# Retention attention and a two-layer FFN on one core: both matrix products by one level of Strassen, with attention and weight rounding as a first part

## The chip, the core and the metric

The kernel runs on one core of a Trainium2 chip. A core has a matrix engine (TensorE, PE in the profile; its weight loads are listed apart as PEld), a vector engine (VectorE, DVE), a scalar engine (ScalarE, ACT), GpSimd (POOL) and a queue that only issues transfers (SyncE, SP). Operands lie in SBUF, matrix results in PSUM: 8 banks of 512 fp32 values in each of 128 partitions. The metric is the device time of one execution in microseconds.

## The reference, cut to what matters

The inputs q, k, v are float32 of 8 batches x 8 heads x 576 positions x 64. The two weight matrices reach the kernel as 8-byte doubles, and the kernel rounds them to float32 itself.

```python
scores = scale * np.matmul(q, k.transpose(0, 1, 3, 2))        # scale = 1/8
gamma = 1.0 - 2.0 ** (-5.0 - np.arange(H))                    # one decay per head
Dmat = np.where(rel >= 0, gamma[:, None, None] ** rel, 0.0)   # rel = i - j
attn_out = np.matmul(scores * Dmat[None], v)
x = attn_out.transpose(0, 2, 1, 3).reshape(B * S, H * D)      # 4608 x 512
h = x @ w_in                                                  # 512 x 2048
sp = np.maximum(h, 0.0) + np.log1p(np.exp(-np.abs(h)))        # softplus
g = h * erf(sp)
return g @ w_out                                              # 2048 x 512
```

## The kernel before

**Attention.** Each batch is cut into pieces of 128 positions (four full ones and one of 64): 40 pieces, 32 full and 8 short. For a piece, `transposes` brings q and k into [feature, position] form by TensorE and copies them out with ScalarE; `scores` makes the 8 heads' score blocks and VectorE multiplies them with a triangle into `sT`; `outputs` makes scores x v, adds the part of earlier positions by a running state (`old`, 128 x 128 per pair of heads), scales the result by the decays into a column block of `xT`, and updates the state by k^T v with two or three VectorE operations (L275 to L278). GpSimd weighs the next piece's keys (L193).

**FFN.** Tokens are taken in 9 chunks of 512. For a chunk, `hidden` (L304) makes h^T in 8 groups of two 128-row tiles of d_ff: per tile 4 float32 products, 128 x 128 weights against 512 columns, into half of a 2-bank PSUM tile `ph`. `serf` (L316) applies Softplus and Erf on ScalarE (each with its own table load) and the product with h on VectorE. `project` (L326) makes the output of the *previous* chunk, 128 tokens at a time, again with 512 columns per product. A float32 product is two MATMUL and two LDWEIGHTS instructions on TensorE: 9 chunks x 64 products x 2 = 1152 records for each of the two matrix products.

**Weight rounding.** The doubles come in 32 parts of 128 x 512 (512 KB each, four in flight). A part costs two ScalarE, five VectorE (L159 to L170) and two GpSimd operations (L171, L172).

**The order of the work** is the program's own, each engine's queue in the order of the code. Pieces 0 to 3 come first, with the first parts of w_in. Then for each chunk c and group g four quarters run: half of `hidden` of chunk c, a step of `project` of chunk c-1, and after each quarter `attend` issues the stages of attention that are due for chunk c+1. The rest of w_in is rounded in chunk 0 and all of w_out by the start of chunk 1. So attention, rounding and matrix products share the engines for the first chunks, and attention and products to the end.

Of the kernel before, what the change touches and what calls it, by code (L numbers as in the profile page):

```python
# [18 lines left out]
P = 128  # L19
# [3 lines left out]
CONST_COLS = H + 2 * NP * P + P  # L23
# [7 lines left out]
def decays():  # L31


    gamma = 1.0 - 2.0 ** (-5.0 - np.arange(H, dtype=np.float64))
    t = np.arange(P)
    gk = gamma[None, :] ** (-t[:, None])
    row = gamma.reshape(NP, 2).repeat(D, axis=1).T
    gq = row[:, :, None] ** t[None, None, :] / math.sqrt(D)
    same = (t[:, None] // D) == (t[None, :] // D)
    gs = (row**P)[:, :, None] * same[:, None, :]  # L40
    tri = t[None, :] >= t[:, None]
    return np.concatenate([gk, gq.reshape(P, -1), gs.reshape(P, -1), tri], axis=1).astype(np.float32)
# [3 lines left out]
def kernel(  # L46
# [13 lines left out]
    TCH = 512  # L60
    n_ch = n_tok // TCH
    n_dc = D_MODEL // P
    n_ft = D_FF // P
    GF = 2
    n_g = n_ft // GF
    W = GF * TCH
    PREFETCH = 2
    WP = 512
    WAHEAD = 4

    const = ctx.enter_context(tc.tile_pool(name="const", bufs=1))
    raw = ctx.enter_context(tc.tile_pool(name="raw", bufs=PREFETCH + 2))
    att = ctx.enter_context(tc.tile_pool(name="att", bufs=2))
    xpool = ctx.enter_context(tc.tile_pool(name="xpool", bufs=3))
    gpool = ctx.enter_context(tc.tile_pool(name="gpool", bufs=12))
    opool = ctx.enter_context(tc.tile_pool(name="opool", bufs=2))
    ps_at = ctx.enter_context(tc.tile_pool(name="ps_at", bufs=2, space=PSUM))
    ps_h = ctx.enter_context(tc.tile_pool(name="ps_h", bufs=2, space=PSUM))
    ps_o = ctx.enter_context(tc.tile_pool(name="ps_o", bufs=1, space=PSUM))
# [4 lines left out]
    loaded = {}  # L84

    def load(i):
        if i >= len(pieces):
            return
        b, s0, n = pieces[i]
        t = {}  # L90
        for name, src in (("k", k), ("q", q), ("v", v)):
            t[name] = raw.tile([P, H, D], FP32, tag=name, name=f"raw_{name}")
            nc.sync.dma_start(out=t[name][:n], in_=src[b, :, s0 : s0 + n, :].rearrange("h p d -> p h d"))
        loaded[i] = t

    load(0)
    cst = const.tile([P, CONST_COLS], FP32, name="cst")
    nc.scalar.dma_start(out=cst, in_=consts)
    gk = cst[:, 0:H]
    gq = cst[:, H : H + NP * P].rearrange("p (a i) -> p a i", a=NP)  # L100
    gs = cst[:, H + NP * P : H + 2 * NP * P].rearrange("p (a i) -> p a i", a=NP)
    tri = cst[:, H + 2 * NP * P : CONST_COLS]
    for i in range(1, PREFETCH):
        load(i)


    w_in_sb = const.tile([P, n_dc, D_FF], FP32, name="w_in_sb")
    w_out_sb = const.tile([P, n_ft, D_MODEL], FP32, name="w_out_sb")

    def parts_in(g):  # L110

        f = g * GF * P
        step = WP // (GF * P)
        for dc in range(0, n_dc, step):
            src = w_in[dc * P : (dc + step) * P, :].rearrange("(c p) f -> p c f", p=P)
            yield w_in_sb[:, dc : dc + step, f : f + GF * P], src, slice(f, f + GF * P)

    def parts_out(g):
        for ft in range(g * GF, (g + 1) * GF):
            src = w_out[ft * P : (ft + 1) * P, :].rearrange("(c p) f -> p c f", p=P)  # L120
            yield w_out_sb[:, ft : ft + 1, :], src, slice(0, D_MODEL)

    parts = [p for g in range(n_g) for p in parts_in(g)] + [p for g in range(n_g) for p in parts_out(g)]
    N_IN = len(parts) // 2
    words = []
    rounded = [0]

    def load_weights():
        if len(words) < len(parts):
            dst, src, cols = parts[len(words)]  # L130
            t = None
            if w_in.dtype == FP32:
                nc.sync.dma_start(out=dst, in_=src[:, :, cols])
            else:
                t_f = gpool.tile([P, W], FP32, tag="g", name="wraw")
                t = t_f[:, :].bitcast(UINT32).rearrange("p (c f) -> p c f", c=dst.shape[1])
                nc.sync.dma_start(out=t, in_=src[:, :, 2 * cols.start : 2 * cols.stop])
            words.append(t)

    def round_weights(upto):  # L140


        while rounded[0] < min(upto, len(parts)):
            n = rounded[0]
            rounded[0] += 1
            dst = parts[n][0]
            t = words[n]
            if t is None:
                load_weights()
                continue  # L150
            pairs = t.rearrange("p c (f two) -> p c f two", two=2)
            pairs_f = t.bitcast(FP32).rearrange("p c (f two) -> p c f two", two=2)
            low, high = pairs[:, :, :, 0], pairs[:, :, :, 1]
            r_f, high_f = pairs_f[:, :, :, 0], pairs_f[:, :, :, 1]
            a_f, a = dst, dst.bitcast(UINT32)
            nc.scalar.activation(a_f, high_f, AF.Abs)
            nc.scalar.mul(out=r_f, in_=low, mul=2.0**-52)

            nc.vector.tensor_scalar(  # L159
                out=a_f, in0=a_f, scalar1=HIGH_LEAST, scalar2=HIGH_MOST, op0=ALU.max, op1=ALU.min  # L160
            )
            nc.vector.tensor_scalar(  # L162
                out=a, in0=a, scalar1=3, scalar2=0x7FFFFFFF, op0=ALU.logical_shift_left, op1=ALU.bitwise_and
            )
            nc.vector.scalar_tensor_tensor(  # L165
                out=a, in0=high, scalar=0x80000000, in1=a, op0=ALU.bitwise_and, op1=ALU.bitwise_or
            )
            nc.vector.tensor_scalar(out=a, in0=a, scalar1=0x40000000, scalar2=None, op0=ALU.bitwise_xor)

            nc.vector.tensor_scalar(out=high, in0=a, scalar1=0xFF800000, scalar2=None, op0=ALU.bitwise_and)  # L170
            nc.gpsimd.tensor_tensor(out=r_f, in0=high_f, in1=r_f, op=ALU.mult)  # L171
            nc.gpsimd.tensor_tensor(out=a_f, in0=a_f, in1=r_f, op=ALU.add)  # L172
            load_weights()

    for _ in range(WAHEAD):
        load_weights()

    ident = const.tile([P, P], FP32, name="ident")
    make_identity(nc, ident)


    xts = {}
    live = {}
    state = {"prev": None}
# [4 lines left out]
    def weigh_keys(i):  # L189

        if i < len(pieces):
            n, t = pieces[i][2], loaded[i]["k"]
            nc.gpsimd.tensor_tensor(  # L193
                out=t[:n], in0=t[:n], in1=gk[:n].unsqueeze(2).to_broadcast([n, H, D]), op=ALU.mult
            )

    def transposes(i):
        n = pieces[i][2]
        t = live[i] = loaded.pop(i)
        load(i + PREFETCH)  # L200
        weigh_keys(i + 1)
        for name in "qk":
            pt = ps_at.tile([P, NP, P], FP32, tag="at", name=f"pt_{name}")
            for p in range(NP):
                nc.tensor.transpose(pt[:, p, :n], flat(t[name][:n, 2 * p : 2 * p + 2, :]), ident[:n, :n])  # L205
            t[name + "T"] = att.tile([P, NP, P], FP32, tag=name + "T", name=name + "T")
            nc.scalar.copy(out=t[name + "T"][:, :, :n], in_=pt[:, :, :n])  # L207

    def scores(i):
        n, t = pieces[i][2], live[i]  # L210
        sT = t["sT"] = att.tile([P, 2, NP, P], FP32, tag="sT", name="sT")
        ps = [ps_at.tile([P, NP, P], FP32, tag="at", name=f"s{e}") for e in range(2)]
        for p in range(NP):
            for e in range(2):
                r = slice(e * D, (e + 1) * D)
                nc.tensor.matmul(  # L216
                    ps[e][:n, p, :n], lhsT=t["kT"][r, p, :n], rhs=t["qT"][r, p, :n], start=True, stop=True
                )
        for e in range(2):
            nc.vector.tensor_tensor(  # L220
                out=sT[:n, e, :, :n],
                in0=ps[e][:n, :, :n],
                in1=tri[:n, :n].unsqueeze(1).to_broadcast([n, NP, n]),
                op=ALU.mult,
            )

    def outputs(i):
        b, s0, n = pieces[i]
        t = live.pop(i)
        old = state["prev"] if s0 > 0 else None  # L230
        o = ps_at.tile([P, NP, P], FP32, tag="at", name="o")
        for p in range(NP):
# [20 lines left out]
        while t0 < b * S + s0 + n:  # L253
            c = t0 // TCH
            if c not in xts:
                xts[c] = xpool.tile([P, n_dc, TCH], FP32, tag="xT", name="xT")
# [144 lines left out]
```

## Time and profile before

| | |
|---|---|
| Median of 3 runs | 1274.95 us (1272.73 to 1275.04) |
| The profiled execution: its time | 1274.32 us |
| Its span, from first to last instruction | 1272.3 us, so 2.0 us lie outside |
| TensorE busy | 1199.3 us (94%) |
| VectorE / ScalarE / GpSimd busy | 305.2 / 429.8 / 121.0 us |
| Moved by DMA | 55.8 MB, of it 45.68 MB read |
| Mean granted TensorE clock | 0.975 of 2.4 GHz |

Busy time is a share of the span over stages that differ; TensorE's busy time also holds the drain of each instruction, so the distance between two starts, not the duration of one, is what an instruction costs in a stream. The view by stretches (below) tells the stages apart.

### The profile page before, as it was taken

To read this page: it belongs to the slowest core of one execution; us is meant where nothing else is said; L and a number is where in the kernel's file an instruction comes from. 1 tells how busy PE (TensorE), PEld (TensorE's weight loads), DVE (VectorE), ACT (ScalarE), POOL (GpSimd) and SP (SyncE) were. 2 spreads that over 40 slices of the span, in tenths; PEclk is the share of its full clock that TensorE was granted. 3 is DMA by queue.
4 is the path that set the end of the run, shared out by engine and by line. 5 is a ranking of instruction groups with operands and counts; after the bars stand their busy time and mean duration, and the time that the engine had idled before them with its cause. 6 is when DMAs were issued, how large, how long until landed. Compare 5 with 4: busy or idle time off the path is not lost.

```text
span 1272.3 us, 10583 instructions
## 1 busy us (share of the span) xinstructions
PE 1199.3 (94%) x4416; PEld 601.2 (47%) x4416; DVE 305.2 (24%) x412; ACT 429.8 (34%) x469; POOL 121.0 (10%) x110
## 2 busy tenths in 40 slices
PE   5966559999999999999999999999999999999998
PEld 4533334454544544445544554445454454444443
DVE  3379975111111111111211111111111111110000
ACT  2355353333323333333332333333323333243210
POOL 3245543000000000000000000000000000000000
PEclk9887779999999999999999999999999999999999
DMA  9723450001202120101130112011211000000000
GB/s 239 180 75 112 124 127 12 7 25 37 51 4 54 25 53 14 42 13 42 25 67 13 42 25 58 9 30 25 58 34 29 0 17 1 17 1 16 1 18 32
DMA packets 124543, 55.80 MB, mean 44 GB/s; under 512 B 113616, under 2 KB 113616, under 8 KB 124496
## 3 DMA queue, kind: packets, MB, share of 16 engines
q1 hardware_dynamic: 124352, 54.54, 17.2%
q8 instruction: 35, 0.57, 0.2%
q10 hardware_dynamic: 144, 0.59, 0.1%
q14 instruction: 12, 0.10, 0.0%
HBM read 45.68 MB, written 9.44 MB: 43 GB/s over the span
## 4 chain that ended last, share of the span: by engine, by line
PE 85%; DVE 6%; ACT 1%; issue 0%; DMA 0%; POOL 0%; DVEq 0%; ACTq 0%; POOLq 0%
PE po L334 39%; PE ph L308 35%; PE s L216 3%; PE o L234 2%; PE o L244 2%; PE kv L270 2%; DVE w_out_sb L165 1%; PE pt_q L205 1%; PE pt_k L205 1%; DVE w_in_sb L165 1%; DVE w_out_sb L162 1%; DVE w_in_sb L162 1%; DMA wraw<-in_moe_w_out_dram 0%; DVE wraw L170 0%; DVE w_out_sb L159 0%
## 5 line engine op out<-in xcount | busy, mean ns | idle before, releaser
L308 PE MATMUL ph<-xT,w_in_sb 128*128 128x512 f32 x1152 | 530.2, 604 | 20.4 <-DVE xT L259 11.4
L334 PE MATMUL po<-w_out_sb,g 128*128 128x512 f32 x1152 | 518.2, 595 | 0.5 <-ACT osb L343 0.5
L308 PEld LDWEIGHTS ph<-xT,w_in_sb 128*128 128x128 f32 x1152 | 216.9, 193 | 271.2 <-issue 247.0
L334 PEld LDWEIGHTS po<-w_out_sb,g 128*128 128x128 f32 x1152 | 215.7, 190 | 260.9 <-issue 256.9
L320 DVE TENSOR_TENSOR g<-ph,g 128x1024 f32<-128x1024 f32 x72 | 88.2, 1224 | 762.4 <-ACT g L319 623.1
L318 ACT ACTIVATE g<-ph 128x1024 f32<-128x1024 f32 x72 | 73.8, 1024 | 491.2 <-PE ph L308 487.4
L318 ACT ACT_TABLE_LOAD x72 | 92.4, 1283 | 68.5 <-issue 33.0
L193 POOL TENSOR_TENSOR raw_k<-raw_k,cst 128x512 f32<-128x512 f32 (+1 forms) x40 | 42.7, 1071 | 746.7 <-DMA raw_k<-in_k_dram 746.7
L207 ACT COPY qT<-pt_q 128x512 f32<-128x512 f32 (+1 forms) x40 | 21.6, 541 | 216.1 <-PE pt_q L205 216.1
L319 ACT ACT_TABLE_LOAD x72 | 92.4, 1283 | 1.3
L319 ACT ACTIVATE g<-g 128x1024 f32<-128x1024 f32 x72 | 76.1, 1056 | 0.8
L216 PE MATMUL s<-qT,kT 64*128 64x128 f32 (+1 forms) x640 | 48.8, 286 | 21.7 <-DVE xT L259 20.1
L216 PEld LDWEIGHTS s<-qT,kT 64*128 64x128 f32 (+1 forms) x640 | 40.1, 187 | 51.0 <-issue 25.0
L220 DVE TENSOR_TENSOR sT<-s,cst 128x512 f32<-128x512 f32 (+1 forms) x80 | 46.9, 627 | 46.4 <-PE s L216 46.4
L205 PE MATMUL pt_q<-ident,raw_q 128*128 128x128 f32 (+1 forms) x160 | 24.8, 280 | 24.9 <-DVE sT L220 18.1
L234 PEld LDWEIGHTS o<-sT,raw_v 128*64 128x64 f32 (+1 forms) x640 | 33.1, 140 | 29.4 <-issue 25.8
L171 POOL TENSOR_TENSOR wraw<-wraw 128x512 f32<-128x512 f32 x32 | 34.4, 1076 | 107.2 <-issue 61.4
L234 PE MATMUL o<-sT,raw_v 128*64 128x128 f32 (+1 forms) x640 | 42.2, 275 | 1.1 <-ACT qT L207 1.0
L259 DVE TENSOR_TENSOR xT<-o,cst 128x512 f32<-128x512 f32 (+1 forms) x44 | 25.6, 590 | 71.0 <-PE o L244 60.1
L205 PEld LDWEIGHTS pt_q<-ident,raw_q 128*128 128x128 f32 (+1 forms) x160 | 19.2, 148 | 46.5 <-DVE sT L220 21.0
L343 ACT COPY osb<-po 128x512 f32<-128x512 f32 x36 | 19.6, 581 | 55.2 <-PE po L334 55.2
L244 PE MATMUL o<-qT,state 128*128 128x128 f32 (+1 forms) x256 | 37.6, 291 | 0.0
(31 smaller groups left out, 404.6 us busy)
## 6 DMA issues: line engine op xcount, KB each, us to landing
out_dram<-osb SPq DMA_DIRECT2D x36, 256.0 KB, 2.2
raw_k<-in_k_dram SPq DMA_DIRECT2D x32, 256.0 KB, 3.7
raw_q<-in_q_dram SPq DMA_DIRECT2D x32, 256.0 KB, 4.4
raw_v<-in_v_dram SPq DMA_DIRECT2D x32, 256.0 KB, 4.3
wraw<-in_moe_w_in_dram SPq DMA_DIRECT2D x16, 512.0 KB, 5.2
wraw<-in_moe_w_out_dram SPq DMA_DIRECT2D x16, 512.0 KB, 3.2
raw_k<-in_k_dram SPq DMA_DIRECT2D x8, 128.0 KB, 2.9
raw_q<-in_q_dram SPq DMA_DIRECT2D x8, 128.0 KB, 3.5
```

The costliest lines, as they stand in the source:

```text
L171: nc.gpsimd.tensor_tensor(out=r_f, in0=high_f, in1=r_f, op=ALU.mult)
L193: nc.gpsimd.tensor_tensor(out=t[:n], in0=t[:n], in1=gk[:n].unsqueeze(2).to_broadcast([n, H, D]), op=ALU.mult)
L205: nc.tensor.transpose(pt[:, p, :n], flat(t[name][:n, 2 * p : 2 * p + 2, :]), ident[:n, :n])
L216: nc.tensor.matmul(ps[e][:n, p, :n], lhsT=t["kT"][r, p, :n], rhs=t["qT"][r, p, :n], start=True, stop=True)
L220: nc.vector.tensor_tensor(out=sT[:n, e, :, :n], in0=ps[e][:n, :, :n], in1=tri[:n, :n].unsqueeze(1).to_broadcast([n, NP, n]), op=ALU.mult,)
L234: nc.tensor.matmul(o[e * D : (e + 1) * D, p, :n], lhsT=t["v"][:n, 2 * p + e, :], rhs=t["sT"][:n, e, p, :n], start=(p == 0), stop=(old is N ...
L244: nc.tensor.matmul(o[:, p, :n], lhsT=old[:, p, :], rhs=t["qT"][:, p, :n], start=False, stop=(p == NP - 1), skip_group_check=True,)
L308: nc.tensor.matmul(ph[:, j * TCH : (j + 1) * TCH], lhsT=w_in_sb[:, dc, f : f + P], rhs=xts[c][:, dc, :], start=(dc == 0), stop=(dc == n_dc ...
L318: nc.scalar.activation(t, ph, AF.Softplus)
L319: nc.scalar.activation(t, t, AF.Erf)
L320: nc.vector.tensor_tensor(out=t, in0=ph, in1=t, op=ALU.mult)
L334: nc.tensor.matmul(po[tt], lhsT=t[:, j * TCH + tt * P : j * TCH + (tt + 1) * P], rhs=w_out_sb[:, ft, :], start=(ft == 0), stop=(ft == n_ft ...
```

## The change

**Strassen.** Each matrix product is split into 2 x 2 blocks and made with 7 block products in place of 8, in the form with 15 block sums (Winograd's), where partial sums stay in PSUM from one block product to the next. For h^T the blocks are halves of d_model and of d_ff against halves of d_model and halves of the chunk's 512 tokens; for the output they are halves of d_ff, of the tokens and of the 512 output columns. All matrix instructions thereby have 256 columns. For a chunk and each of 4 groups the first product has 7 block products of 4 float32 products each; the second has 7 block products of 16. That is 9 x (4 x 28 + 112) = 2016 float32 products of 256 columns, 4032 MATMUL records, for 1152 float32 products of 512 columns, 2304 records.

The sums of weight blocks (`wa`, `wb`, 7 each) are made once, at rounding, by 4 VectorE operations for each block position (16 of 512 values and 32 of 256 a partition). The sums of x are made once per chunk (4 VectorE operations), the sums of the left operand of the second product once per group (`finish_group`, 4 after the two products with the Erf result).

**Two parts.** Attention for all 40 pieces and the rounding of all 32 parts come first, in three stages one piece apart, with 0.84 parts of rounding per piece; x^T is stored chunk by chunk to DRAM (`xd`, 1 MB each) and SBUF and PSUM are given to the second part. That part loads one chunk of x^T at a time (one buffer, `load_x`), and runs `first_products`, `middle_products`, `last_products`, `serf`, `finish_group` and `multiply2` as the loop at the end writes them. The state of attention now accumulates in PSUM (`kv`) with absolute decays on v and on the output, and ScalarE copies it out; VectorE's state operations and the exclusive-or of the rounding are gone.

```diff
     TCH = 512
+    TH = TCH // 2
...
-    GF = 2
...
+    OH = D_MODEL // 2
+    GP = 2
+    n_g = n_fp // GP
...
-            nc.vector.tensor_scalar(out=a, in0=a, scalar1=0x40000000, scalar2=None, op0=ALU.bitwise_xor)
...
+                load_weights()
+                if sums:
+                    sums[0](*sums[1:])
...
+        def store(upto):
+            while stored[0] < upto:
+                nc.sync.dma_start(out=xd[stored[0]], in_=xts.pop(stored[0]))
+                stored[0] += 1
...
+        for i in range(n_p + 2):
+            if i < n_p:
+                transposes(i)
+            if 0 <= i - 1 < n_p:
+                scores(i - 1)
+            if i >= 2:
+                b, s0, _ = pieces[i - 2]
+                store((b * S + s0) // TCH)
+                outputs(i - 2)
+            round_weights(-(-len(todo) * (i + 1) // (n_p - 2)))
+        store(n_ch)
...
+    def multiply1(c, g, a, acc, start):
+        for j in range(GP):
+            f = (g * GP + j) * P
+            for d in range(2):
+                nc.tensor.matmul(
+                    acc[:, j * TH : (j + 1) * TH],
+                    lhsT=wa[:, a, d, f : f + P],
+                    rhs=x[c][a][:, d, :],
...
+    def first_products(c, g):
...
+        multiply1(c, g, A11, t["a"], True)
+        nc.scalar.copy(out=t["g1"][:, 0], in_=t["a"])
+        multiply1(c, g, A12, t["e"], True)
+        tt(t["g1"][:, 0], t["e"], t["g1"][:, 0], ALU.add)
+
+    def middle_products(c, g):
...
+        multiply1(c, g, S2, t["a"], False)
+        nc.vector.tensor_copy(out=t["g1"][:, 1], in_=t["a"])
+        multiply1(c, g, S3, t["g"], True)
+        multiply1(c, g, S1, t["a"], False)
+        nc.vector.tensor_copy(out=t["g2"][:, 1], in_=t["a"])
+        tt(t["g2"][:, 1], t["g"], t["g2"][:, 1], ALU.add)
+
+    def last_products(c, g):
...
+        multiply1(c, g, S4, t["a"], False)
+        nc.scalar.copy(out=t["g2"][:, 0], in_=t["a"])
+        multiply1(c, g, A22, t["g"], False)
+        tt(t["g1"][:, 1], t["g"], t["g1"][:, 1], ALU.add)
+
+    def serf(c, g):
...
+        for func in (AF.Softplus, AF.Erf):
+            for j in "12":
+                nc.scalar.activation(t["e" + j], t["g" + j] if func == AF.Softplus else t["e" + j], func)
+
+    def finish_group(c, g):
...
+        for j in "12":
+            tt(t["g" + j], t["g" + j], t["e" + j], ALU.mult)
...
+        tt(s1, g12, g22, ALU.add)
+        tt(s2, s1, g11, ALU.subtract)
+        tt(g12, g11, g12, ALU.subtract)
+        tt(s4, g21, s2, ALU.subtract)
...
+    for c in range(n_ch):
+        for g in range(n_g):
+            middle_products(c, g)
+            if g > 0:
+                finish_group(c, g - 1)
+            if g + 1 < n_g:
+                first_products(c, g + 1)
+            else:
+                acc, osb = begin_outputs(c)
+                multiply2(c, B11, acc["a"], True, ALL[: n_g - 2])
+            last_products(c, g)
+            serf(c, g)
+        finish_group(c, n_g - 1)
+        multiply2(c, B11, acc["a"], False, ALL[n_g - 2 : n_g - 1])
+        multiply2(c, B21, acc["e"], True, ALL[: n_g - 1])
+        load_x(c + 1)
+        multiply2(c, B11, acc["a"], False, ALL[n_g - 1 :])
...
+        multiply2(c, B21, acc["e"], False, ALL[n_g - 1 :])
...
+        multiply2(c, T2, acc["a"], False, ALL)
...
+        multiply2(c, T3, acc["g"], True, ALL)
+        multiply2(c, T1, acc["a"], False, ALL)
...
+        if c + 1 < n_ch:
+            first_products(c + 1, 0)
+        multiply2(c, B22, acc["a"], False, ALL)
...
+        multiply2(c, T4, acc["g"], False, ALL)
```

On TensorE, in the middle of the kernel before, a quarter's product (`ph`, 4 products of 512 columns), a step of the previous chunk's output (`po`) and a stage of attention (`o`, `kv`) take turns:

```order
L308 MATMUL ph<-xT,w_in_sb 128x512 x4
L334 MATMUL po_2776<-w_out_sb,g 128x512 x2
L334 MATMUL po_2779<-w_out_sb,g 128x512 x2
L234 MATMUL o<-sT,raw_v 64x128 x8
L244 MATMUL o<-qT,state 128x128 x4
L270 MATMUL kv<-raw_v,raw_k 128x128 x4
L308 MATMUL ph<-xT,w_in_sb 128x512 x4
```

In the changed kernel's second part the same engine has block products alone, here of the groups of one chunk (`acc_a`, `acc_e`, `acc_g` are the PSUM sums, `xs` the sums of x):

```order
L362 MATMUL acc_a<-x,wa 128x256 x4
L362 MATMUL acc_e<-x,wa 128x256 x4
L362 MATMUL acc_a<-x,wa 128x256 x4
L362 MATMUL acc_g<-xs,wa 128x256 x4
L362 MATMUL acc_a<-xs,wa 128x256 x4
L362 MATMUL acc_g<-xs,wa 128x256 x4
```

Attention has left these rows, and each accumulator is written again four to sixteen matrix instructions after it was last read or written.

On ScalarE, before, one group's Softplus and Erf stand like this; the table load of Softplus waits for VectorE (a buffer of `g` to come free), the operation itself for TensorE's `ph`:

```order
L318 ACT_TABLE_LOAD [waits DVE_49]
L318 ACTIVATE g<-ph 128x1024 [waits PE_49]
L319 ACT_TABLE_LOAD
L319 ACTIVATE g<-g 128x1024 [waits Activation_49]
```

In the changed kernel, one group of the second part:

```order
L401 COPY g_2986<-acc_a 128x512 [waits DVE_49,PE_49]
L410 ACT_TABLE_LOAD [waits DVE_49]
L410 ACTIVATE e_3073<-g_2985 128x1024 [waits Activation_49]
L410 ACTIVATE e_3074<-g_2986 128x1024 [waits Activation_49]
L410 ACT_TABLE_LOAD
L410 ACTIVATE e_3073<-e_3073 128x1024 [waits Activation_49]
L410 ACTIVATE e_3074<-e_3074 128x1024 [waits Activation_49]
```

The input of Softplus now comes from VectorE (the sum that ends `last_products`), and the wait for it stands at the table load, not behind it.

On TensorE at the seam of the two products of a chunk, changed kernel, with what the first instruction of each waits for (`g_3157` is the last group's left operand, `oa` and `oe` the sums of the output):

```order
L432 MATMUL oa<-wb,g_3051 128x256 x4
L362 MATMUL acc_a<-x,wa 128x256 [waits DVE_49]
L362 MATMUL acc_a<-x,wa 128x256 x3
L362 MATMUL acc_g<-xs,wa 128x256 [waits DVE_49]
L362 MATMUL acc_g<-xs,wa 128x256 x3
L432 MATMUL oa<-wb,g_3104 128x256 [waits DVE_49]
L432 MATMUL oa<-wb,g_3104 128x256 x3
L432 MATMUL oe<-wb,g_2985 128x256 x4
L432 MATMUL oe<-wb,g_3051 128x256 x4
L432 MATMUL oe<-wb,g_3104 128x256 x4
L432 MATMUL oa<-wb,g_3157 128x256 [waits DVE_49]
```

Between the last group's first product (`acc_g`) and the first instruction that reads this group's result (`oa<-wb,g_3157`) there stand 16 float32 products.

## Rows read from the trace of the kernel before

**Rows 1.** The page: span, and busy time of the engines.

```profile
span 1272.3 us, 10583 instructions
PE 1199.3 (94%) x4416; PEld 601.2 (47%) x4416; DVE 305.2 (24%) x412; ACT 429.8 (34%) x469; POOL 121.0 (10%) x110
```

**Rows 2.** Stretches: us, busy (count) per engine, granted clock, DMA share, GB/s.

```profile
core 0: us, PE busy (x) PEld busy (x) DVE busy (x) ACT busy (x) POOL busy (x), PEclk, DMA share, GB/s
20.00:40.00 20.00, 16.08 (x143) 12.83 (x139) 13.54 (x24) 3.90 (x7) 7.61 (x7) 0.97 0.91 202
40.00:60.00 20.00, 19.18 (x90) 11.83 (x91) 6.79 (x12) 7.45 (x10) 4.33 (x5) 0.86 0.78 207
...
100.00:120.00 20.00, 14.16 (x69) 8.94 (x70) 18.76 (x28) 7.53 (x13) 9.68 (x8) 0.73 0.37 102
...
300.00:600.00 300.00, 300.00 (x1126) 149.74 (x1125) 51.16 (x66) 99.45 (x105) 10.40 (x10) 1.00 0.14 33
```

**Rows 3.** Groups by line: records, busy us, mean ns, idle time before.

```profile
L308 PE MATMUL ph<-xT,w_in_sb 128*128 128x512 f32 x1152 | 530.2, 604 | 20.4 <-DVE xT L259 11.4 <-POOL w_in_sb L172 9.0
L334 PE MATMUL po<-w_out_sb,g 128*128 128x512 f32 x1152 | 518.2, 595 | 0.5 <-ACT osb L343 0.5
```

**Rows 4.** Timeline of the weight loads: start, us, line, idle before.

```profile
607.97 0.97 PEld L270 LDWEIGHTS kv<-raw_v,raw_k 128*128 128x128 f32 x8
...
612.41 0.19 PEld L308 LDWEIGHTS ph<-xT,w_in_sb 128*128 128x128 f32 x1 [0.24 <-issue]
612.84 0.19 PEld L308 LDWEIGHTS ph<-xT,w_in_sb 128*128 128x128 f32 x1 [0.24 <-issue]
```

**Rows 5.** Timeline of TensorE's matrix instructions in the middle.

```profile
607.09 1.16 PE L244 MATMUL o<-qT,state 128*128 128x128 f32 x8
608.08 1.06 PE L270 MATMUL kv<-raw_v,raw_k 128*128 128x128 f32 x8
608.98 3.60 PE L334 MATMUL po<-w_out_sb,g 128*128 128x512 f32 x8
...
615.94 1.16 PE L216 MATMUL s<-qT,kT 64*128 64x128 f32 x16
```

**Rows 6.** Timeline of TensorE over the opening pieces.

```profile
24.82 0.66 PE L205 MATMUL pt_q<-ident,raw_q 128*128 128x128 f32 x4 [0.58 <-DVE sT L220]
...
31.80 0.66 PE L205 MATMUL pt_q<-ident,raw_q 128*128 128x128 f32 x4 [0.58 <-DVE sT L220]
...
37.61 2.02 PE L216 MATMUL s<-qT,kT 64*128 64x128 f32 x16 [1.34 <-DVE xT L259]
...
43.17 2.08 PE L244 MATMUL o<-qT,state 128*128 128x128 f32 x8
```

**Rows 7.** DMA queues: packets, MB, their time as share of 16 engines' span.

```profile
q1 hardware_dynamic: 124352, 54.54, 17.2%
```

**Rows 8.** Groups by line and shape, VectorE and GpSimd.

```profile
L320 DVE TENSOR_TENSOR g<-ph,g 128x1024 f32<-128x1024 f32 x72 | 88.2, 1224 | 762.4 <-ACT g L319 623.1 <-PE po L334 139.2
L172 POOL TENSOR_TENSOR w_in_sb<-w_in_sb,wraw 128x512 f32<-128x512 f32 x16 | 21.7, 1355 | 1.3
L278 DVE TENSOR_TENSOR state<-state,cst 128x512 f32<-128x512 f32 x24 | 16.8, 700 | 0.8
L168 DVE TENSOR_SCALAR w_in_sb<-w_in_sb 128x512 uint32<-128x512 uint32 x16 | 6.8, 427 | 0.5
```

**Rows 9.** Timeline of TensorE after a pause at 124 us.

```profile
126.07 1.75 PE L216 MATMUL s<-qT,kT 64*128 64x128 f32 x16 [2.11 <-DVE xT L259]
127.75 5.35 PE L308 MATMUL ph<-xT,w_in_sb 128*128 128x512 f32 x8
```

**Rows 10.** Timeline of ScalarE over one group in the middle.

```profile
599.96 1.28 ACT L318 ACT_TABLE_LOAD   x1
606.17 1.02 ACT L318 ACTIVATE g<-ph 128x1024 f32<-128x1024 f32 x1 [4.93 <-PE ph L308]
...
608.50 1.06 ACT L319 ACTIVATE g<-g 128x1024 f32<-128x1024 f32 x1
```

**Rows 11.** Timeline of the end.

```profile
1268.13 0.59 ACT L343 COPY osb<-po 128x512 f32<-128x512 f32 x1 [1.13 <-PE po L334]
```

More of the change, by code (lines that the diff above doesn't have):

```diff
@@ L73 @@
[L73 to L79, printed above, removed]
+    wa = const.tile([P, 7, 2, D_FF // 2], FP32, name="wa")
@@ L80 @@
+    A11, A12, S3, A22, S1, S2, S4 = range(7)
+    wb = const.tile([P, 7, n_fp, OH], FP32, name="wb")
+    B11, T3, B21, B22, T1, T2, T4 = range(7)
+    xd = [dram.tile([P, n_dc, TCH], FP32, tag="xd", name="xd") for _ in range(n_ch)]
     ctx.enter_context(tc.manual_schedule())
     pieces = [(b, s0, min(P, S - s0)) for b in range(B) for s0 in range(0, S, P)]
[L84 to L167, printed above, removed]
-            nc.vector.tensor_scalar(out=a, in0=a, scalar1=0x40000000, scalar2=None, op0=ALU.bitwise_xor)
[L170 to L173, printed above, removed]
@@ L209, in scores @@
[L209 to L215, printed above, removed]
-                nc.tensor.matmul(
[L217 to L225, printed above, removed]
@@ new lines, with load_x @@
+    ps_2 = ctx.enter_context(tc.tile_pool(name="ps_2", bufs=1, space=PSUM, reuse_waits="tile"))
+    x = {}
+    def load_x(c):
+        if c >= n_ch:
+            return
+        t = xpool.tile([P, n_dc, TCH], FP32, tag="x", name="x")
+        nc.sync.dma_start(out=t, in_=xd[c])
+        s = xpool.tile([P, 4, 2, TH], FP32, tag="xs", name="xs")
+        b11, b12, b21, b22 = (t[:, 2 * d : 2 * d + 2, h * TH : (h + 1) * TH] for d in range(2) for h in range(2))
+        t1, t2, t3, t4 = (s[:, j] for j in range(4))
+        tt(t1, b12, b11, ALU.subtract)
+        tt(t2, b22, t1, ALU.subtract)
+        tt(t3, b22, b12, ALU.subtract)
+        tt(t4, b21, t2, ALU.subtract)
+        x[c] = {A11: b11, A12: b21, S4: b22, A22: t4, S1: t1, S2: t2, S3: t3}
@@ L266, in outputs @@
-        if s0 + n < S:
-            kv = ps_at.tile([P, NP, P], FP32, tag="at", name="kv")
-            for p in range(NP):
-                h = slice(2 * p, 2 * p + 2)
-                nc.tensor.matmul(
-                    kv[:, p, :], lhsT=flat(t["k"][:n, h, :]), rhs=flat(t["v"][:n, h, :]), start=True, stop=True
-                )
-            new = att.tile([P, NP, P], FP32, tag="state", name="state")
-            if old is None:
-                nc.vector.tensor_tensor(out=new, in0=kv, in1=gs, op=ALU.mult)
-            else:
-                nc.vector.tensor_tensor(out=new, in0=kv, in1=old, op=ALU.add)
-                nc.vector.tensor_tensor(out=new, in0=new, in1=gs, op=ALU.mult)
-            state["prev"] = new
@@ L282 @@
-    stages = [(transposes, 0)]
-    for i in range(len(pieces)):
-        stages.append((scores, i))
-        if i + 1 < len(pieces):
-            stages.append((transposes, i + 1))
-        stages.append((outputs, i))
-    done = [0]
-    def stages_for(tokens):
-        last = max(i for i, (b, s0, _) in enumerate(pieces) if b * S + s0 < tokens)
-        return stages.index((outputs, last)) + 1
-    def attend(upto):
-        while done[0] < min(upto, len(stages)):
-            of, i = stages[done[0]]
-            of(i)
-            done[0] += 1
@@ L302 @@
-    gs_of = {}
-    def hidden(c, g, js, ph):
-        for j in js:
-            f = (g * GF + j) * P
-            for dc in range(n_dc):
-                nc.tensor.matmul(
-                    ph[:, j * TCH : (j + 1) * TCH],
-                    lhsT=w_in_sb[:, dc, f : f + P],
-                    rhs=xts[c][:, dc, :],
-                    start=(dc == 0),
-                    stop=(dc == n_dc - 1),
-                )
-    def serf(c, g, ph):
-        t = gs_of[c, g] = gpool.tile([P, W], FP32, tag="g", name="g")
-        nc.scalar.activation(t, ph, AF.Softplus)
-        nc.scalar.activation(t, t, AF.Erf)
-        nc.vector.tensor_tensor(out=t, in0=ph, in1=t, op=ALU.mult)
@@ L347 @@
[L347 to L370 removed]
+    W = GP * TH
@@ new lines, in multiply2 @@
+    def multiply2(c, a, acc, start, gs):
+        for g in gs:
+            left = groups[c, g]["left"][a]
+            for j in range(GP):
+                for tp in range(2):
+                    nc.tensor.matmul(
+                        acc[:, tp, :],
+                        lhsT=left[:, j * TH + tp * P : j * TH + (tp + 1) * P],
+                        rhs=wb[:, a, g * GP + j, :],
+                        start=(start and g == 0 and j == 0 and tp == 0),
+                        stop=(g == n_g - 1 and j == GP - 1),
+                        skip_group_check=True,
+                    )
```

361 lines of the change are left out of this document (245 added, 116 removed).

## The prediction

> **What bounds the kernel now.** I read the page's busy times first, then the stretches, then the timelines of TensorE and its weight loads. The page says TensorE 94% busy, the next engine a third [rows 1]. The stretches say where the rest is: from 300 to 600 us TensorE is busy for all 300 us at full clock, while in the opening it had 16.1 and 19.2 of 20 us, and at 100 us 14.2 of 20 at a granted 0.73 of 2.4 GHz beside a VectorE busy for 18.8 [rows 2]. So in the steady state TensorE's instruction stream is the time, and over the first chunks VectorE's rounding and waits for attention hold it.
>
> What an instruction costs in the stream is the distance of two starts. Weight loads of the FFN stand 0.43 us apart (612.41, 612.84), 0.19 busy and 0.24 idle [rows 4]; a run of 8 lasts 3.60 with its drain [rows 5]. With 1152 records in each product [rows 3], the FFN needs 2304 x 0.43 = 991 us of TensorE. The other 1272.3 - 991 = 281 us are attention's matrix instructions (busy 1199.3 - 530.2 - 518.2 = 151 us [rows 1, 3]), slow clock and idle time.
>
> **The matrix products.** 2304 records of 512 columns go, 4032 of 256 columns come. No row has 256 columns, so I bound it. From below it is half of 0.43, 0.215 us, if only columns count. From above it is twice a 128-column instruction: 8 of them lie 0.99 us apart (607.09 to 608.08), 0.124 each, which gives 0.248 [rows 5]. The next 8 take 0.90 (608.08 to 608.98), 0.112 each, with weight loads end to end for 0.97 us, 0.12 a load [rows 4, 5]. So at 128 columns loads and columns are near level, and at 256 the load has twice the room. The straight line from 0.112 at 128 to 0.43 at 512 gives 0.218 at 256; the lower bound 0.215. I take 0.217: 4032 x 0.217 = 875 us, with ends of 867 and 1000. That is 116 less than now.
>
> A load of 0.12 to 0.19 us hides behind 0.21 us of columns only if loads run beside matrix instructions that use the whole array. In the FFN's rows they do: 0.43 is 512 columns and no more, load included [rows 4]. The Trainium skill says otherwise ("TensorE: Matmul & The Clock Gate", section "Measured speedup vs the span model"): weight loads overlap matrix instructions in flight only where the row group differs. All products here use all rows, so by that rule 0.43 would have been load plus columns, and the trace differs. What the rule would make of the time is the third rival.
>
> **The first part.** All of attention and rounding now run without FFN under them. Its resources, by rows:
> - DMA: before, the hardware queue moved 54.54 MB in 17.2% of the span, 219 us, 249 GB/s with all engines at work [rows 7]. The first part moves as much: the same 45 MB of input, and 9.4 MB of x^T where 9.4 MB of output was. At the 202 and 207 GB/s of the busy opening [rows 2] it is 266 us. I take the middle, 245.
> - VectorE: 305.2 - 88.2 (L320) = 217 us belong to attention and rounding now [rows 1, 8]. Off go 56 state operations at 0.70 and 32 exclusive-ors at 0.43 (39 + 14); on come the weight sums, 16 at 0.70 and 32 of half the width at 0.35 (11 + 11). That leaves 186 us. At 12 places the sums wait for GpSimd to finish the part just rounded, two operations of up to 1.36 [rows 8]: 12 x 2.7 = 32. Together 218.
> - TensorE: 151 us at the clock it had. GpSimd 121 us as now [rows 1].
>
> Four engines within 120 to 245 us, so the slowest sets it if the queues don't make them take turns. Now a piece takes 7.0 us (24.82 to 31.80) because its stages follow each other [rows 6]; the new loop has scores one piece and outputs two pieces behind, so a wait for a copy or for the triangle has a whole piece to pass. Behind a late VectorE sum stands the next triangle, and TensorE waits for that one piece later; that is the coupling I see, and 245 against 218 leaves it some room. The last load is followed by two pieces' stages, some 13 us. First part: 245 + 13 = 258, with ends of 219 + 13 = 232 and 40 x 7.0 + 13 = 293, or worse with a slow clock (second rival).
>
> **The seam of the parts.** The last 1 MB of x^T goes out, the first comes back, nothing beside it: 2.1 MB at 249 GB/s is 8.4, and 9 with VectorE's last operation. Then TensorE starts at half clock: after a pause of 2.11 us 16 score instructions took 1.75 us and 8 FFN ones 5.35, where 1.16 and 3.60 are usual [rows 5, 9]. That is 2.4; I take 3.
>
> **Waits in the second part.** One group is 28 products, 56 records, 12.15 us of TensorE. Beside it VectorE has nine 512-element operations (0.70 each) and two of 1024 (1.22 each) [rows 8], 8.8 us; ScalarE two table loads of 1.28, four operations of 1.02 to 1.06 [rows 10] and two copies of 0.59 [rows 11], 8.0 us. Neither fills the group, but they form a ring: last sum from PSUM (0.7), table load, two Softplus, table load, first Erf (1.28 + 2.05 + 1.28 + 1.06 = 5.7), two products and four sums (about 4.5, since independent ones overlap), the next group's first sum (0.65), the last sum again. With some 0.3 for hand-overs it is 11.9 us against 12.15. TensorE does not wait inside a chunk, by a small margin.
>
> At the chunk's seam it does. Before, the Softplus table load was done at 599.96 while TensorE still worked, 4.9 us ahead of its input [rows 10]; now the order puts the wait for the input at the table load, so its 1.28 us comes after. From the end of the last group's first product: 0.25 drain, 0.7 sum, 5.7 on ScalarE, 1.22 product, 0.3 hand-overs, 8.2 us until the first left operand is there. TensorE has 16 products, 32 x 0.217 = 6.9 us. It waits 1.3 us per chunk, nothing with a free table load. A pause may cost clock as well: after 1.34 us the scores took 2.02 where 1.16 is usual [rows 5, 6]; after 0.58 it did not fall [rows 6]. I take 2.0 per chunk, 9 x 2 = 18, with ends of 0 and 9 x 3.7 = 33. The load of the next x and its four sums (8 us of DMA and VectorE) lie under 70 us of second products; exposed, they would add 9 x 8 = 72 us.
>
> **The end.** The last instruction is followed by a copy and a transfer as now: the last copy starts at 1268.13, 4.2 before the end [rows 1, 11]. With a transfer of twice the size, 5.
>
> **The sum.** 258 + 9 + 3 + 875 + 18 + 5 = 1168 us of span. The profiled execution took 1274.32 for a span of 1272.3, so 2 us lie outside, and the forecast is 1170 us. The profiled execution stands 0.6 below the median of 1274.95. The gain is the products' 116 us; the rest costs 293 us for the 281 of now. So attention no longer runs under a full TensorE, and that gives back about 12.
>
> **Rivals.**
> 1. *Everything lies well.* Transfers at 249 GB/s (232 for the first part), 867 for the products, no wait at the seams: 232 + 9 + 3 + 867 + 0 + 5 + 2 = 1118. For it: loads are deep in the queue. Against: from 20 to 60 us the opening held 202 and 207, not 249 [rows 2]. 12%.
> 2. *The first part is a chain, or runs at half clock.* With gaps of 0.6 to 1.3 us per piece the clock fell at 37.6 and 43.2 us (8 state instructions 2.08, where 1.16 is usual) [rows 5, 6]. Double 151 us is 302, + 13 = 315; at 7.0 us a piece 293. The total is 1205 to 1227, say 1216. For it: TensorE has 151 us of work in 258. Against: at half clock it would be busier, which brings the clock back. 17%.
> 3. *Slower: the stream of short instructions is paced by its weight loads.* If each 256-column instruction costs two 128-column ones, 0.248, the products take 1000 us and the total is 1295. The decision lies at 0.217 + (1274 - 1170) / 4032 = 0.243 us an instruction. For it: loads are already end to end at 128 columns [rows 4]. Against: 0.12 a load leaves half of 0.217 free. 6%. If loads did not overlap at all, 0.215 + 0.12 = 0.335, the products would take 1351 and the total be 1646; the rows of 0.43 speak against it, 1%. That last case is the rule of the Trainium skill named above.
> 4. *The ring of ScalarE and VectorE sets the second part.* It is 0.25 us short of TensorE's group. If VectorE's operations from SBUF alone take a fifth more, the ring is 12.9: 0.75 over 36 groups and 1 us more at 9 seams, 36 us, 1206. 12%.
>
> **Chances and range.** The forecast holds 52%, between 1145 and 1195. I count as no change what lies within 0.2%, 2.5 us. All but rival 3 are faster; the cases of rival 3 that come out near 0.243 are the few for "same". Faster 0.90, same 0.03, slower 0.07. The range 1130 to 1235 takes in rivals 2 and 4 and leaves out most of rivals 1 and 3.
>
> **What would show it.** In the profile after: weight loads of the second part 0.215 to 0.22 us apart, TensorE's clock at 1.00 there; a first part of about 258 us in which the DMA share is near 0.9 and x^T is written; ScalarE's Softplus table load directly before Softplus with the wait ahead of it; one TensorE pause of 1 to 2 us per chunk, released by VectorE's product with Erf. I am wrong if the starts lie over 0.23 us apart, if the first part is over 300 us, or if TensorE pauses inside the groups.

## The result: faster, 1186.8 us for 1273.8

The changed kernel takes 1186.76 us (median of 4, 1184.73 to 1189.41), the kernel before, in the same comparison, 1273.84 us: a ratio of 0.932, interval 0.929 to 0.934. The forecast was 1170. The gain is 87 us where 105 were forecast; the profiled execution has a span of 1186.5 us.

The page of the changed kernel, to be read against [rows 1] (span, then busy time of each engine):

```profile
span 1186.5 us, 14961 instructions
...
PE 1092.2 (92%) x6400; PEld 950.7 (80%) x6400; DVE 510.6 (43%) x721; ACT 403.2 (34%) x533; POOL 120.4 (10%) x110
```

TensorE's busy time fell by 107 us although its records rose from 4416 to 6400. VectorE's rose by 205 us, all of it in the second part (338 us there, below), beside a TensorE that is busy for 875 of 888 us.

Three stretches of the changed kernel: the first part, the seam, the second part (columns as in [rows 2]):

```profile
0.00:290.20 290.20, 216.91 (x2368) 184.00 (x2368) 171.84 (x261) 105.14 (x209) 120.42 (x110) 0.83 0.82 190
290.20:298.10 7.90, 0.04 (x2) 0.01 (x1) 0.45 (x2) 0.00 (x0) 0.00 (x0) 0.62 0.75 265
298.10:1186.50 888.40, 875.26 (x4032) 766.68 (x4032) 338.35 (x459) 298.01 (x324) 0.00 (x0) 1.00 0.06 21
```

The second part is near the forecast: full clock, 4032 records, 888 us where 3 + 875 + 18 + 5 = 901 were forecast. The first part is not: 290 us, with TensorE busy for 217, DMA for 0.82 and VectorE for 172. No engine fills it.

TensorE at the start of the second part and in its course (timeline; start, us, records):

```profile
298.10 3.78 PE L362 MATMUL acc_a<-x,wa 128*128 128x256 f32 x8 [7.86 <-DMA x<-xd]
301.67 2.23 PE L362 MATMUL acc_e<-x,wa 128*128 128x256 f32 x8
303.74 1.89 PE L362 MATMUL acc_a<-xs,wa 128*128 128x256 f32 x8
305.47 1.89 PE L362 MATMUL acc_g<-xs,wa 128*128 128x256 f32 x8
307.19 1.89 PE L362 MATMUL acc_a<-xs,wa 128*128 128x256 f32 x8
```

After the pause of 7.86 us at the seam the first eight records start over 3.57 us and the next over 2.07, then every eight over 1.73: 0.216 an instruction, 2.2 us lost to the clock. [Rows 4 and 5] gave the ends of 0.215 and 0.248 for this; 0.216 is the end at which columns alone set the pace. The weight loads are busy for 767 of the 888 us, and at most 0.001 us of each is seen in the pace. The rule of the Trainium skill that was weighed in the prediction ("TensorE: Matmul & The Clock Gate"; it stands in the section "The mechanism") lets a load overlap only where the row group differs, and would have exposed each of these loads. The trace differs. The same section also names a load into a background weight buffer as one that is pulled ahead; whether that is the case here, no run shows.

What TensorE waited for, over the whole span (engine, line, what it waited for: total us, times, longest):

```profile
PE pt_q L232 <- DMA raw_q<-in_q_dram: 39.1, 18, 8.1
PE s L245 <- DVE sT L143: 23.6, 10, 4.7
PE oa L432 <- DVE g L143: 7.9, 9, 0.9
```

The third line is the chunk's seam, 0.9 us nine times. The first two are the first part: q arrives late, and the triangle on VectorE is late. The queues of SyncE and VectorE tell why. SyncE's own waits in the first part:

```profile
SPq L167 <- POOL wa L199: 34.5, 14, 5.1
...
SPq L167 <- POOL wb L199: 24.6, 11, 3.9
SPq L167 <- DVE wraw L197: 22.2, 10, 4.9
```

L167 is the transfer of a weight part; it needs the buffer that the rounding has just used, and its 81 us of waits (59 for GpSimd, 22 for VectorE) stand ahead of the next piece's q, k and v. VectorE around 105 us:

```profile
105.18 0.43 DVE L197 TENSOR_SCALAR wraw<-wa 128x512 uint32<-128x512 uint32 x1
105.52 2.93 DVE L143 TENSOR_TENSOR wa<-wa 128x512 f32<-128x512 f32 x3
110.74 1.52 DVE L143 TENSOR_TENSOR wa<-wa 128x512 f32<-128x512 f32 x1 [2.29 <-POOL wa L199]
112.18 1.21 DVE L143 TENSOR_TENSOR sT<-s,cst 128x1024 f32<-128x1024 f32 x1
```

The fourth weight sum waits 2.29 us for GpSimd, and the triangle (`sT`) stands behind it.

### The profile page after: what moved, and what is told of

Read it like the earlier page. It is cut to its first block, busy times and chain, and to the rows that moved or that the text cites. A ratio compares the mean times of both kernels' runs of the same rounds, so it can differ in the third digit from the quotient of the medians.

```text
span 1186.5 us, 14961 instructions
## 1 busy us (share of the span) xinstructions
PE 1092.2 (92%) x6400; PEld 950.7 (80%) x6400; DVE 510.6 (43%) x721; ACT 403.2 (34%) x533; POOL 120.4 (10%) x110
## 4 chain that ended last, share of the span: by engine, by line
PE 75%; DMA 7%; ACT 5%; DVE 5%; POOL 3%; issue 2%; SPq 1%; ACTq 0%; POOLq 0%; DVEq 0%
PE acc_a L362 21%; PE oa L432 20%; PE acc_g L362 10%; PE og L432 10%; PE acc_e L362 5%; ACT e L410 2%; PE s L245 2%; DMA raw_k<-in_k_dram 2%; DMA raw_q<-in_q_dram 2%; PE o L261 2%; DVE g L143 1%; PE oe L432 1%; DMA raw_v<-in_v_dram 1%; PE o L271 1%; POOL wraw L198 1%
## 5 line engine op out<-in xcount | busy, mean ns | idle before, releaser
L432 PE MATMUL oa<-wb,s 128*128 128x256 f32 x864 | 191.0, 379 | 0.7 <-ACT osb L477 0.7
L432 PEld LDWEIGHTS oa<-wb,s 128*128 128x128 f32 x864 | 164.1, 190 | 23.3 <-ACT osb L477 1.1
L362 PE MATMUL acc_a<-x,wa 128*128 128x256 f32 x576 | 138.0, 383 | 7.9 <-DMA x<-xd 7.9
L362 PE MATMUL acc_a<-xs,wa 128*128 128x256 f32 x576 | 136.1, 379 | 0.0
L362 PE MATMUL acc_g<-xs,wa 128*128 128x256 f32 x576 | 136.1, 379 | 0.0
L362 PEld LDWEIGHTS acc_a<-x,wa 128*128 128x128 f32 x576 | 110.4, 192 | 23.2 <-DMA x<-xd 8.0
L432 PE MATMUL og<-wb,g 128*128 128x256 f32 x576 | 127.3, 379 | 0.0
L362 PEld LDWEIGHTS acc_a<-xs,wa 128*128 128x128 f32 x576 | 109.4, 190 | 14.9
L362 PEld LDWEIGHTS acc_g<-xs,wa 128*128 128x128 f32 x576 | 109.4, 190 | 14.9
L432 PEld LDWEIGHTS og<-wb,g 128*128 128x128 f32 x576 | 109.4, 190 | 14.9
```

The lines of the kernel that those rows point to most:

```text
L362: nc.tensor.matmul(acc[:, j * TH : (j + 1) * TH], lhsT=wa[:, a, d, f : f + P], rhs=x[c][a][:, d, :], start=(start and j == 0 and d == 0), ...
L432: nc.tensor.matmul(acc[:, tp, :], lhsT=left[:, j * TH + tp * P : j * TH + (tp + 1) * P], rhs=wb[:, a, g * GP + j, :], start=(start and g = ...
```

## The experiments

Three theories of the first part went into the first three runs; the fourth is about the chunk's seam. A: the transfers' rate sets its 290 us. B: SyncE's queue is held by the rounding, so that q, k, v are issued late. C: VectorE's sums wait for GpSimd and hold the triangle. All ratios are to runs of the kernel before on the same chip; the differences below are of medians against 1186.8.

**Weight transfers issued a step later, a part fewer ahead.** A transfer now goes out just before the next part is rounded, not right behind the rounding of the last one:

```diff
             while rounded[0] < min(upto, len(todo)):
+                if rounded[0] > 0:
+                    load_weights()
                 dst, _, sums = todo[rounded[0]]
...
-                load_weights()
                 if sums:
```

> The transfer of weight part n+3 is issued before part n is rounded (into the buffer of part n-1), where the changed kernel issues part n+4 after it; so SyncE's queue has no fresh GpSimd operation to wait for, and q, k, v of later pieces stand behind it no longer. Theory A (the first part of 290 us is set by the rate of its transfers, DMA share 0.86): under 5 us, 1183 to 1190. Theory B (SyncE's queue is held by the rounding: 81 us of waits at the weight transfers, and TensorE then waits 46 us for q and k): 15 to 30 us less, 1157 to 1172. Theory C (VectorE's sums wait for GpSimd and hold the triangle): under 5 us.

Measured: 1174.13 us, ratio 0.922 (0.920 to 0.923), 12.6 less. Theory A expected under 5, B 15 to 30: B's sign, just under its size. SyncE's waits at the weight transfers only fell from 81 to 59 us, so its queue was not free yet. And TensorE's waits changed places:

```profile
PE s L246 <- DVE sT L143: 56.2, 16, 5.8
PE pt_q L233 <- DMA raw_q<-in_q_dram: 15.2, 3, 8.1
```

The wait for q fell from 39 to 15 us, the one for the triangle rose from 24 to 56.

**x^T (the attention output, which the first part stores) stored twice.**

```diff
             while stored[0] < upto:
+                nc.sync.dma_start(out=xd2[stored[0]], in_=xts[stored[0]])
                 nc.sync.dma_start(out=xd[stored[0]], in_=xts.pop(stored[0]))
```

> Each chunk of x^T is stored to DRAM a second time (9.4 MB more in the first part; the copy is not read). Theory A (transfers set the first part): 9.4 MB at the 200 GB/s of that part are 47 us, 1225 to 1240. Theories B and C (queues set it, the transfers have room of 0.14): 0 to 15 us, 1187 to 1202.

Measured: 1196.79 us, ratio 0.939 (0.938 to 0.941), 10.0 more, where theory A asked for 38 or more. A falls: the first part takes a sixth more traffic for 10 us, 2.4 of them at the seam, whose pause grew from 7.9 to 10.3.

**Weight sums a piece later.**

```diff
-                    sums[0](*sums[1:])
+                    waiting.append(sums)
...
+            sum_weights()
             round_weights(-(-len(todo) * (i + 1) // (n_p - 2)))
+        sum_weights()
         store(n_ch)
```

> The 12 sets of weight sums are issued one piece later, after the next piece's triangle and x^T, when GpSimd is through with the part. Theory C (VectorE waits 25 us for GpSimd at the sums, and TensorE's scores 24 us for the triangle behind it): 10 to 25 us less, 1162 to 1177. Theories A and B: under 6 us.

Measured: 1170.05 us, ratio 0.919 (0.917 to 0.921), 16.7 less, as C expected. Again the other wait grew, here that for q:

```profile
PE pt_q L238 <- DMA raw_q<-in_q_dram: 51.0, 17, 8.2
...
PE s L251 <- DVE sT L143: 3.0, 3, 1.5
```

**One more group of products at the chunk's seam.**

```diff
-                multiply2(c, B11, acc["a"], True, ALL[: n_g - 2])
+                multiply2(c, B11, acc["a"], True, ALL[: n_g - 3])
...
-        multiply2(c, B11, acc["a"], False, ALL[n_g - 2 : n_g - 1])
+        multiply2(c, B11, acc["a"], False, ALL[n_g - 3 : n_g - 1])
```

> One group of the output's first block product (4 products, 1.73 us of TensorE) moves from before the last group's first product to behind it, so that 20 in place of 16 products cover the way over ScalarE and VectorE. The nine waits of 0.9 us (7.9 us by the profile) go: 1179, if each wait is on the path and nothing else is late; 1187 if TensorE then waits as long for the copy that frees the accumulator (1.0 us after the middle products, now covered by 1.73 us).

Measured: 1179.87 us, ratio 0.926 (0.924 to 0.927), 6.9 less. The line of the seam's wait:

```profile
PE oa L432 <- DVE g L143: 2.0, 9, 0.2
```

Of 7.9 us 5.9 went, as the first value of the expectation has it, and the second part is 882.5 us for 888.4, so nothing came in their place; the remaining 1 us of the difference is within what medians of this kernel scatter.

**The three edits together.**

> The three edits together: weight transfers issued a part later, weight sums a piece later, one more group of the output at the seam. Alone they took 12.6, 16.7 and 6.9 us off. In the first the wait for the triangle grew from 24 to 56 us, in the second the wait for q from 39 to 51, so each edit laid the other's wait bare. Theory B with C (two queues hold each other up): both waits go, the first part falls from 290 to 255 to 262 us, 1140 to 1152. Theory A' (with the queues free the transfers set it after all, near 0.95 busy): the two edits of the first part overlap, 1155 to 1165.

Measured: 1132.08 us, ratio 0.888 (0.887 to 0.890), 54.7 less than the changed kernel, though the edits alone add up to 36.2. Theory A' falls, and B with C has the right sign but too small a size: the time is 8 us below its 1140. The two queues do hold each other up: each edit alone left more of the other's wait. The stretches:

```profile
0.00:239.40 239.40, 192.05 (x2368) 165.06 (x2368) 184.39 (x261) 104.53 (x209) 121.44 (x110) 0.91 1.03 231
239.40:247.25 7.85, 0.01 (x1) 0.00 (x0) 0.44 (x2) 0.00 (x0) 0.00 (x0) 0.60 0.74 267
247.25:1129.60 882.35, 875.10 (x4032) 766.55 (x4032) 337.56 (x459) 297.93 (x324) 0.00 (x0) 1.00 0.06 21
```

The first part is 239.4 us, 50.8 less in the two profiled executions (by the medians, 54.7 less the 5.9 of the seam, 49), at a DMA share of 1.03 and 231 GB/s in place of 0.82 and 190. SyncE's waits at weight transfers:

```profile
SPq L173 <- POOL wa L207: 7.2, 7, 2.6
...
SPq L173 <- POOL wb L207: 2.7, 4, 0.8
```

In all they are 13 us, where the changed kernel had 81 and each edit alone still had 59 and 66. The expectation had both waits of TensorE go; they only shrank, from 39 to 28 us for q and from 24 to 14 for the triangle:

```profile
PE pt_q L239 <- DMA raw_q<-in_q_dram: 28.2, 10, 8.3
...
PE s L252 <- DVE sT L143: 14.1, 11, 2.8
```

TensorE's waits tell only half of it. The first parts of the run with late transfers and of the one with late sums:

```profile
0.00:274.93 274.93, 202.34 (x2368) 176.06 (x2368) 176.96 (x261) 103.61 (x209) 121.28 (x110) 0.85 0.87 201
0.00:269.39 269.39, 199.14 (x2368) 167.02 (x2368) 179.67 (x261) 105.45 (x209) 120.55 (x110) 0.89 0.88 205
```

TensorE's idle time in the first part (length less busy time) was 73.3 us in the changed kernel, 72.6 and 70.3 with one edit, and 47.4 with all three. Its busy time for the same 2368 records went from 216.9 to 202.3, 199.1 and 192.1, with a granted clock of 0.83, 0.85, 0.89 and 0.91. So what one edit alone gained stands nearly all in TensorE's busy time, and only both together took idle time away: of the 50.8 us, 25 are busy time and 26 idle time. Busy time times clock, a rough estimate of the work at full clock, is 172 to 180 us in all four, so the busy time goes with the clock. The same 16 score instructions of the changed kernel, once with no pause just ahead of them and once soon after pauses of 2.8 and 0.6 us, show the two levels:

```profile
118.16 1.16 PE L245 MATMUL s<-qT,kT 64*128 64x128 f32 x16
...
125.97 2.08 PE L245 MATMUL s<-qT,kT 64*128 64x128 f32 x16
```

So a wait that the queues leave can cost TensorE twice, by its length and by the clock behind it; no run sets the two apart.

**The same with x^T stored twice** (the edit of the second experiment on top).

> The version with the three edits, and each chunk of x^T stored a second time (9.4 MB; the copy is not read). With the queues held (before the edits) the same store cost 10 us. Theory A' (with the queues free the transfers set the first part, 240 to 250 GB/s): 9.4 MB at 245 GB/s are 38 us, 1165 to 1172. Theory D (VectorE, busy for 190 of 240 us, sets it now): under 15 us, 1132 to 1147.

Measured: 1150.98 us, ratio 0.903 (0.901 to 0.905), 18.9 more, where the same store had cost 10.0 with the queues held. That is between the two: less than the 38 us of the rate alone, more than the 15 of a first part that VectorE sets; 2.5 of the 18.9 stand at the seam, where the pause is 10.4 us for 7.85. The stretch from 100 to 200 us, with the three edits alone and with the second store beside them:

```profile
100.00:200.00 100.00, 83.42 (x1053) 71.61 (x1050) 85.96 (x125) 47.27 (x94) 56.01 (x49) 0.91 1.11 252
100.00:200.00 100.00, 80.26 (x1002) 69.15 (x998) 78.19 (x116) 44.16 (x89) 49.98 (x45) 0.87 1.07 265
```

So more bytes went through per microsecond than without the second store: 265 GB/s for 252 in this stretch, 247 for 231 over the whole first part. The expectation's 245 GB/s was near that rate; its fault was to price the store as if the first part had no room, where the last 39 us of it moved 156 GB/s in the run with the three edits. TensorE's wait for q rose from 28 to 43 us. With the queues free, transfers are therefore the likeliest limit of the first part; this is argued and not shown, and how much of it is TensorE's (192 of 239 us) or VectorE's (184) was not taken apart.

**Two parts without Strassen.** The first part has as many operations as in the changed kernel, the second has the plain products of 512 columns:

```diff
-    multiply1(c, g, A11, t["a"], True)
...
+            slot = ((A11, A12), (S3, A22))[half][dc // 2]
+            nc.tensor.matmul(
+                ph[:, j * TCH : (j + 1) * TCH],
+                lhsT=wa[:, slot, dc % 2, col : col + P],
+                rhs=xs[c][:, dc, :],
```

> The first part as in the changed kernel, with as many operations (two of the weight sums go to another place, so that the plain weights remain), the second part with the plain products of the kernel before: 2304 instructions of 512 columns, chunk c+1's first product between chunk c's second. Theory S (the gain is the seventh product less and nothing else): 298 + 2304 x 0.43 = 991 + 5, some 1294 to 1300, so slower than before by 20 to 26 us and 108 to 113 slower than with Strassen. Rival (the gain is the two parts, which keep attention and rounding out of TensorE's way): under 1274.

Measured: 1296.3 us, ratio 1.018 (1.016 to 1.019): slower than before by 21.8 us, and 109.5 slower than with Strassen, both as theory S has it. The rival, that the two parts alone make the gain, falls. TensorE's lines hold the same 1152 records each as in [rows 3], and the second part starts where the changed kernel's does:

```profile
298.05 12.54 PE L356 MATMUL ph<-x,wa 128*128 128x512 f32 x22 [7.90 <-DMA x<-xd]
```

**Columns per instruction, in the kernel before.** The same products, cut into two instructions of 256 columns, or four of 128, each with its own weight load:

```diff
-                    rhs=xts[c][:, dc, :],
+                    rhs=xts[c][:, dc, n0 : n0 + 256],
...
-                    rhs=w_out_sb[:, ft, :],
+                    rhs=w_out_sb[:, ft, n0 : n0 + 256],
```

> The kernel before with each matrix instruction of the FFN cut into two of 256 columns, same weights loaded twice; 4608 records for 2304. If columns set the pace with 0.216 as in the changed kernel: 4608 x 0.216 = 995, 4 us more than 991, so 1277 to 1281. If weight loads pace them (0.248): 150 us more.

> The same cut into four of 128 columns, 9216 records. By the rows of attention, 0.112 to 0.124 an instruction: 1032 to 1143, which is 41 to 152 us more, 1315 to 1426. If columns alone set the pace (0.1075): no change.

Measured: 1278.42 us for 256 columns, ratio 1.0035 (1.0023 to 1.0048), and 1311.16 for 128, ratio 1.029 (1.027 to 1.030): the first inside its 1277 to 1281, the second 4 us below the 1315 of the rows of attention and far from no change. The difference of 36.6 us on 9216 instructions over 991 gives (991 + 37) / 9216 = 0.1115 each at 128 columns, by estimate. There the loads are end to end, 32 in 3.65 us:

```profile
599.86 3.65 PEld L309 LDWEIGHTS ph<-xT,w_in_sb 128*128 128x128 f32 x32
```

**The last chunk's x^T stays in SBUF and is multiplied first**, on top of the three edits:

```diff
-    load_x(0)
-    first_products(0, 0)
+    load_x(n_ch - 1)
+    first_products(n_ch - 1, 0)
...
-    for c in range(n_ch):
+    for c in [n_ch - 1, *range(n_ch - 1)]:
```

> The version with the three edits, and the last chunk's x^T stays in SBUF and is multiplied first, so that the seam of the parts has no way to DRAM and back (1 MB less stored and loaded). The seam was 7.8 us of pause before the first block product, and some 2 us of slow clock behind it. If the pause is on the path: 1122 to 1126. If the sums of x, which the first instruction then waits for, or another wait take its place: 1128 to 1132.

Measured: 1121.04 us, ratio 0.879 (0.877 to 0.881), 11.0 less than the three edits alone and 65.7 less than the changed kernel: the fastest here, and 1 us under the first range of the expectation. TensorE goes from attention into the products without the pause, and without the slow clock behind it:

```profile
238.85 1.10 PE L279 MATMUL o<-qT,state 128*128 128x64 f32 x8 [0.30 <-ACT state L304]
239.80 1.95 PE L375 MATMUL acc_a<-xT,wa 128*128 128x256 f32 x8
241.58 1.89 PE L375 MATMUL acc_e<-xT,wa 128*128 128x256 f32 x8
```

## Why the prediction was right, and where it was not

- *The matrix products: right.* 0.217 an instruction was forecast, 0.216 measured (eight over 1.73 us), in the changed kernel and in the kernel before with 256 columns; 871 us for 875. Rival 3, the slower one, had its condition at 0.243; even at 128 columns an instruction costs 0.1115, so two of them 0.223, short of it.
- *The first part: the step that failed.* The mechanism had its parts (transfers, rounding, sums behind GpSimd, triangle behind the sums), but the step "a wait for a copy or for the triangle has a whole piece to pass" and "245 against 218 leaves it some room" took the queues as apart. Measured: 290 for 258. That this lies inside my ends of 232 and 293 is luck, for the chain that gave the upper end is not the cause. SyncE's queue was missing from that step altogether: the weight transfer waits for the last operations on the part (most of it for GpSimd's), and q, k, v wait behind it. The diff ahead of the prediction has `load_weights` right behind the rounding; I followed VectorE's waits through that loop and not SyncE's. With both queues freed the first part is 239, within the 232 to 258 of the sum by transfers. So the coupling, for which the sum had nothing, was worth some 50 us, and the 258 itself was 19 too many; the two errors cancel in part.
- *TensorE in the first part: the term was too small.* It was put at 151 us and measured 216.9, more than VectorE's 172. The 151 takes the FFN's records off with their drains (530.2 + 518.2); with the 991 us of their starts 1199.3 - 991 = 208 remain, FFN products of the slow opening included. The sum did not use the term, but rival 2 was priced and weighed by it.
- *The seam of the parts: right.* 7.9 us for 9, and 2.2 of slow clock for 3.
- *The ring inside the groups: right.* TensorE's list of waits has no line from inside a group; rival 4 did not come. The table load of Softplus stands behind its wait as the order showed:

```profile
328.88 1.28 ACT L410 ACT_TABLE_LOAD   x1 [1.91 <-DVE g L143]
330.18 2.00 ACT L410 ACTIVATE e<-g 128x1024 f32<-128x1024 f32 x2
```

- *The chunk's seam: the place right, the size too high.* 0.9 us per chunk for 1.3, and no clock lost behind it: the products after the pause take 1.99 and 1.89 us for eight, where 1.89 is usual. 7.9 us for 18.

```profile
360.04 1.99 PE L432 MATMUL oa<-wb,g 128*128 128x256 f32 x8 [0.88 <-DVE g L143]
361.87 1.89 PE L432 MATMUL oe<-wb,g 128*128 128x256 f32 x8
```

- *The end:* VectorE's last sum starts at 1182.0, 4.5 us before the end, for 5.
- *The sum.* 32 us too few in the first part; against that 4 too many in the products, 10 at the seams of the chunks, and 2 at the seam of the parts: 16 us, as the span of 1186.5 against 1168 shows within 3 us. Rival 2 (a first part of 293 to 315 at a slow clock or as a chain) came close in time, and half of it in kind. It was no chain of stages: the edits that freed the queues left attention's instructions as they are and took 51 us off. But the slow clock was there, at 0.83 if not at half, and of the 51 us 25 are busy time that went as the clock rose to 0.91. The queues set the pauses; how much the clock alone cost behind them was not tried apart.

That the gain is the block product saved (seven in place of eight) is shown by the plain second part: with it the two parts cost 21.8 us more than the mixed order of before, and Strassen gives 109.5. By the 991 us an eighth of the products is 124; the waits at the chunk's seams (7.9) and the shorter instructions (4) account for most of what is missing.

## What to carry to other kernels

A sum of busy times bounds a stage from below, and each queue that holds work of two kinds can add to it: write down for every queue, the transfer queue too, what stands behind each waiting instruction. Where two queues wait on each other, an edit of one shows less than its worth, since the other's wait grows; try them together before one is dismissed. Look at busy time, too, when a wait is removed: here half of what the freed queues gave was the same instructions running at a higher clock. On TensorE, halving the columns of a float32 product from 512 to 256 cost 0.35% of this kernel, so a block algorithm that saves products pays almost in full.

## What the runs showed of the hardware

- A float32 instruction of 256 columns took 0.216 us and one of 128 columns 0.1115, where half and a quarter of 0.43 are 0.215 and 0.1075. The weight loads, 0.19 us each at 256 columns, ran beside the instructions; at 128 columns they stood end to end, 32 in 3.65 us.
- TensorE's clock stayed at 2.4 GHz through nine pauses of 0.9 us in a dense stream, and was at half (1.2 GHz) for the first 3.6 us after a pause of 7.9.
- In the first part, where pauses are many, the same 2368 records kept TensorE busy for 216.9 us at a mean clock of 0.83 and for 192.1 at 0.91.
- The DMA rate depended on the mix: in the stretch from 100 to 200 us 252 GB/s at a share of 1.11 with the input and one store of x^T, 265 at 1.07 with a second store beside it.
